# Attention and MLP kernel on one core: transposes moved from TensorE to DMA, a third PSUM bank for the MLP, output drained by VectorE, DMA queues in emission order

## The chip, the cores and the metric

The kernel runs on one core of one Trainium2 chip. The metric is device time in microseconds (us). "Before" is the kernel as it was, "after" is the kernel with the change. Before took 579.5 us (median of three runs, 578.33 to 581.34).

Five engines work beside each other, each on its own instruction list: TensorE (PE in the profile), VectorE (DVE), ScalarE (ACT), GpSimd (POOL) and SyncE (SP). (In before the first four were busy 81, 42, 55 and 37% of the span.) SP computes nothing here. It issues transfers to the core's 16 DMA engines. In these traces VectorE and SP work in the order of their lists, and what stands behind a waiting entry waits with it: in after an `xn` whose inputs were there at 62.1 us started at 73.95, behind a `kp` that waited for its own, and SP issued nothing from 62.9 to 74.5 us, while it waited for that `xn`.

## The reference, cut to what matters

```python
def reference(q, k, v, g_q, g_k, w_in, w_out):     # q, k, v: 8 batches, 12 heads, 448 rows, 64 columns
    q_n, k_n = rmsnorm(q, g_q), rmsnorm(k, g_k)
    attn = softmax(q_n @ k_n.T / sqrt(64))
    x = heads_side_by_side(attn @ v)               # 3584 x 768
    h = x @ w_in                                   # w_in 768 x 2048
    g = h * clip(h + 3, 0, 6) / 6
    return g @ w_out                               # w_out 2048 x 768
```

## The kernel before

Heads are worked on in pairs: 6 pairs a batch, 48 in all. For each pair q and k are loaded with sequence rows on the partitions, squared (`sq`, POOL), summed (`ssq`, VectorE), turned into 1/rms (`rs`, ScalarE) and scaled to bf16 (`qks`, POOL). The kernel's score matmul takes q and k with head columns on the partitions, so `qks` is transposed; k is then multiplied by a mask (`kp`, VectorE), so that one matmul sees one head of the pair. After softmax and the matmul with v, the result `x_ps` is normalised (`xn`, VectorE) and transposed once more (`xT`), because the kernel's MLP takes it with model columns on the partitions. The MLP of batch b−1 (`h`) and of batch b−2 (`y`) is interleaved with the attention of batch b, so that TensorE always has something to do.

The parts that the change touches:

```python
    ps_T = pool("ps_T", 1, space=PSUM)      # transposes
    ps_S = pool("ps_S", 3, space=PSUM)      # scores
    ps_X = pool("ps_X", 1, space=PSUM)
    ps_R = pool("ps_R", 1, space=PSUM)
    ps_M = pool("ps_M", 2, space=PSUM)      # MLP, h and y; 8 banks in these pools
    # ... cut
    def trans_pair(P):
        b, j = divmod(P, NPAIR)
        qks = st.pop(("qks", P))
        ps = ps_T.tile([128, 2, NT, 128], BF16, name="t_ps", tag="T")
        for i in range(2):
            for t in range(NT):
                nc.tensor.transpose(
                    ps[:, i, t, :], qks[:, i, t].rearrange("p h d -> p (h d)"), identity[:])
        nc.vector.tensor_copy(
            out=qT_of(b)[:, j, 0:SM], in_=ps[:, 0].rearrange("p t c -> p (t c)"))
        kp = kp_pool.tile([128, 2, SM], BF16, name="kp")
        for a in range(2):
            nc.vector.tensor_scalar_mul(
                kp[:, a, :], ps[:, 1].rearrange("p t c -> p (t c)"), gmask[:, a:a + 1])
    # ... cut
    def xtrans(P):                          # the attention output of pair P
        xn = st.pop(("xn", P))
        ps = ps_T.tile([128, NT, 128], BF16, name="xt_ps", tag="T")
        for t in range(NT):
            nc.tensor.transpose(ps[:, t, :], xn[:, t].rearrange("p a d -> p (a d)"), identity[:])
        nc.vector.tensor_copy(
            out=xT_of(b)[:, j, 0:SM], in_=ps[:].rearrange("p t c -> p (t c)"))
    # ... cut
        if part == 3:                       # end of y_part
            y_sb = y_pool.tile([128, HALF], FP32, name="y_sb")
            nc.scalar.copy(out=y_sb[:], in_=y_ps)
            # then nc.sync.dma_start(out=..., in_=y_sb)
    # ... cut
    def att_items(P):                       # what is emitted while pair P is finished
        n = P + 1
        items = [(0.0, lambda: load_step(P + 5)), (0.0, lambda: prep_step(P + 3)),
                 (0.36, lambda: trans_step(P + 2))]
        sc = [(0.19, lambda u=u: score(n, u)) for u in range(NU)] if n < NP else []
        vs = [(0.3, lambda t=t: av(P, t)) for t in range(NT + 1)]
        items += merge(sc, vs)
        items.append((0.18, lambda: xtrans(P)))
        # ... cut
    def load_w_in():                        # float32 in HBM, cast to bf16 on the way, issued by POOL
        for kt in range(NKT):
            after(nc.gpsimd.dma_start(
                out=w_in_sb[:, kt, :], in_=moe_w_in[kt * 128:(kt + 1) * 128, :]), st["prep", 1])
```

The order of each engine's list is not the order of emission: the framework simulates the program and sorts the instructions of each engine by when it expects them to be ready.

## Time and profile before

| | before |
|---|---|
| time, median | 579.5 us |
| span of the profiled run, granted TensorE clock | 582.8 us, 0.974 |
| first score exponential | 39.9 us |
| batch starts (first exponential of each batch) | 39.9, 72.8, 115.9, 183.5, 255.8, 325.1, 392.5, 452.7 us |
| first exponential of the last pair | 502.5 us |

The batch starts are read from the timeline: ScalarE takes seven exponentials per pair, and each 42nd starts a batch. A batch is thus a natural ruler for this kernel. First the page: busy time and share of each engine, then TensorE and the DMA engines in 40 slices of the span, in tenths.

```profile
PE 469.9 (81%) x3848; PEld 278.2 (48%) x3848; DVE 245.7 (42%) x544; ACT 320.5 (55%) x638; POOL 212.9 (37%) x245
...
PE   0045859877689888888788899888899999999996
...
DMA  8974995462134222212222123222110000010012
```

No engine is full over the whole span, but TensorE is at 9 in the last quarter, where mostly MLP is left, and at 8 in the middle. Some groups of before's instructions (line, engine, operation, tiles, shapes, count; busy us and mean ns; idle time just before them and what ended it):

```profile
L248 PE MATMUL t_ps<-identity,qks 128*128 128x128 bf16 x288 | 26.1, 228 | 44.6 <-POOL qks L165 41.1
...
L379 ACT COPY y_sb<-y_ps 128x384 f32<-128x384 f32 x56 | 26.8, 479 | 44.0 <-PE y_ps L373 43.9
...
L254 DVE TENSOR_SCALAR kp<-t_ps,gmask 128x384 bf16<-128x384 bf16 x96 | 35.2, 409 | 0.0
```

The 228 ns of one transpose is not its cost: matmuls overlap in the pipeline, and the transposes start 56 ns apart, so 504 of them are worth 28 us of TensorE. What VectorE and TensorE of before wait for (us in all, times, longest):

```profile
DVE ssq L159 <- POOL sq L138: 87.3, 37, 5.5
...
DVE qT L250 <- PE t_ps L248: 26.4, 28, 2.8
```

```profile
PE h_ps L356 <- DVE gT_1641 L363: 10.7, 7, 5.1
```

VectorE's longest wait is for the squares; TensorE's own waits, after the 34.7 us before its first transpose, are many and short. The windows view of before, for the first two batches and the batches after them (length, busy time of each engine with counts, granted clock, DMA share, GB/s):

```profile
core 0: us, PE busy (x) PEld busy (x) DVE busy (x) ACT busy (x) POOL busy (x), PEclk, DMA share, GB/s
40.00:73.00 33.00, 25.11 (x264) 16.12 (x263) 18.62 (x45) 25.12 (x54) 29.30 (x33) 0.90 0.77 165
73.00:116.00 43.00, 33.43 (x337) 20.87 (x336) 30.28 (x68) 33.98 (x81) 37.84 (x38) 0.92 0.73 176
116.00:453.00 337.00, 286.99 (x2369) 169.39 (x2368) 152.72 (x335) 197.28 (x391) 128.99 (x138) 0.97 0.26 75
```

In the first two batches the DMA engines are three quarters busy, not least because the weights arrive there; after that they have room.

### The profile page before, as it was taken

How to read it: one execution, taken by the hardware profiler on the slowest of the kernel's cores; microseconds unless marked ns; L12 is line 12 of the kernel's file. 1: busy time of each engine (PE TensorE's matmuls, PEld its weight loads, DVE VectorE, ACT ScalarE, POOL GpSimd, SP SyncE). 2: the span in 40 equal slices, each digit the busy share in tenths (PEclk: the TensorE clock that was granted, in tenths of full speed). 3: DMA queues.
4: the chain of work that ended last, by engine and by line, in shares of the span. 5: the costliest groups of instructions: out<-in, count | busy, mean ns of one | idle time of the engine just before them, and what ended most of it. 6: DMA issues, size and time to landing. Idle time of an engine off the chain costs nothing.

```text
span 582.8 us, 9889 instructions
## 1 busy us (share of the span) xinstructions
PE 469.9 (81%) x3848; PEld 278.2 (48%) x3848; DVE 245.7 (42%) x544; ACT 320.5 (55%) x638; POOL 212.9 (37%) x245
## 2 busy tenths in 40 slices
PE   0045859877689888888788899888899999999996
PEld 0023535543345555544444455555455566654454
DVE  0035658864544453435543443544443434232200
ACT  1055977865566655636555666555667665733221
POOL 5069769974543532324434353223221100000000
PEclk9997998998999999979998999989999999999999
DMA  8974995462134222212222123222110000010012
GB/s 204 231 149 120 201 236 162 132 154 82 55 86 132 82 70 72 93 54 55 62 77 80 56 82 96 73 64 70 55 55 29 29 28 28 28 42 27 28 56 68
DMA packets 69648, 50.98 MB, mean 87 GB/s; under 512 B 22753, under 2 KB 68833, under 8 KB 69601
## 3 DMA queue, kind: packets, MB, share of 16 engines
q1 hardware_dynamic: 63168, 43.27, 26.4%
q0 software_dynamic: 2976, 6.29, 5.8%
q10 hardware_dynamic: 3456, 0.79, 0.7%
q8 instruction: 30, 0.49, 0.3%
q14 instruction: 18, 0.14, 0.1%
HBM read 45.61 MB, written 11.01 MB: 97 GB/s over the span
## 4 chain that ended last, share of the span: by engine, by line
PE 35%; POOL 23%; DMA 19%; DVE 10%; ACT 5%; issue 4%; SPq 4%; POOLq 0%; ACTq 0%
DMA qk<-in_k_dram 15%; PE h_ps L356 14%; PE y_ps L373 13%; POOL qks L165 9%; POOL sq L138 9%; DVE ssq L159 4%; ACT t_sb L361 3%; PE s_ps L270 3%; SPq L190 2%; PE t_ps L248 2%; SPq L145 2%; POOL sqr L138 1%; DMA vr<-in_v_dram 1%; DMA qkr<-in_k_dram 1%; DVE xn L298 1%
## 5 line engine op out<-in xcount | busy, mean ns | idle before, releaser
L271 ACT ACTIVATE eT<-s_ps,zero_c 128x448 bf16<-128x448 f32 x336 | 200.9, 643 | 52.5 <-PE s_ps L270 50.0
L361 ACT ACTIVATE t_sb<-h_ps,half_c 128x384 f32<-128x384 f32 (+1 forms) x128 | 81.1, 634 | 78.2 <-PE h_ps L356 78.0
L356 PEld LDWEIGHTS <-w_in_sb 128*128 128x128 bf16 x768 | 72.5, 98 | 95.5 <-issue 54.9
L165 POOL TENSOR_TENSOR qks<-qk,rs 128x384 bf16<-128x384 f32 x96 | 77.7, 831 | 103.4 <-PE t_ps L248 71.1
L270 PE MATMUL s_ps<-qT,kp 128*128 128x448 bf16 x288 | 97.1, 360 | 2.5 <-DVE kp L254 1.3
L138 POOL TENSOR_TENSOR sq<-qk 128x768 f32<-128x768 f32 x45 | 66.0, 1468 | 88.4 <-DMA qk<-in_k_dram 80.6
L159 DVE TENSOR_REDUCE ssq<-sq 128x12 f32<-128x768 f32 x48 | 45.7, 952 | 95.7 <-POOL sq L138 87.3
L279 PEld LDWEIGHTS <-eT 128*128 128x128 bf16 x1152 | 66.3, 100 | 30.4 <-issue 2.5
L248 PE MATMUL t_ps<-identity,qks 128*128 128x128 bf16 x288 | 26.1, 228 | 44.6 <-POOL qks L165 41.1
L379 ACT COPY y_sb<-y_ps 128x384 f32<-128x384 f32 x56 | 26.8, 479 | 44.0 <-PE y_ps L373 43.9
L248 PEld LDWEIGHTS <-qks 128*128 128x128 bf16 x288 | 20.9, 101 | 54.1 <-POOL qks L165 41.9
L130 ACT ACTIVATE rs<-ssq,eps_c 128x12 f32<-128x12 f32 x48 | 15.0, 313 | 51.9 <-POOL qks L165 37.3
L356 PE MATMUL h_ps<-xT_984,w_in_sb 128*128 128x512 bf16 x96 | 26.6, 394 | 11.3 <-DVE gT_1641 L363 10.7
L270 PEld LDWEIGHTS <-kp 128*128 128x128 bf16 x288 | 27.9, 99 | 16.3 <-DVE kp L254 1.7
L254 DVE TENSOR_SCALAR kp<-t_ps,gmask 128x384 bf16<-128x384 bf16 x96 | 35.2, 409 | 0.0
L356 PE MATMUL h_ps<-xT_2580,w_in_sb 128*128 128x512 bf16 x96 | 26.5, 389 | 6.9 <-DVE gT_3374 L363 6.7
L373 PE MATMUL y_ps<-w_out_sb,gT_1641 128*128 128x384 bf16 x128 | 28.0, 338 | 1.7 <-ACT y_sb L379 1.6
L373 PE MATMUL y_ps<-w_out_sb,gT_3374 128*128 128x384 bf16 x128 | 27.3, 332 | 1.7 <-ACT y_sb L379 1.6
L356 PE MATMUL h_ps<-xT_1757,w_in_sb 128*128 128x384 bf16 x96 | 22.0, 337 | 7.9 <-DVE gT_2459 L363 7.8
L250 DVE COPY qT<-t_ps 128x384 bf16<-128x384 bf16 x48 | 17.0, 355 | 26.6 <-PE t_ps L248 26.4
L298 DVE TENSOR_TENSOR xn<-x_ps,rd 128x384 bf16<-128x384 f32 x48 | 26.7, 555 | 1.2
L336 PE MATMUL xt_ps<-identity,xn 128*128 128x128 bf16 x144 | 17.3, 226 | 12.1 <-DVE xn L298 11.8
(104 smaller groups left out, 745.5 us busy)
## 6 DMA issues: line engine op xcount, KB each, us to landing
qk<-in_q_dram SPq DMA_DIRECT2D x48, 192.0 KB, 2.5
qk<-in_k_dram SPq DMA_DIRECT2D x48, 192.0 KB, 2.8
vf<-in_v_dram SPq DMA_DIRECT2D x48, 192.0 KB, 2.5
out_dram<-y_sb SPq DMA_DIRECT2D x48, 192.0 KB, 1.9
w_in_sb<-in_moe_w_in_dram POOLq DMA_DIRECT2D x6, 512.0 KB, 11.9
w_out_sb<-in_moe_w_out_dram POOLq DMA_DIRECT2D x4, 768.0 KB, 14.2
vr<-in_v_dram SPq DMA_DIRECT2D x16, 96.0 KB, 6.4
out_dram<-y_sb SPq DMA_DIRECT2D x16, 96.0 KB, 2.2
```

The lines of the kernel that those rows point to most:

```text
L138: nc.gpsimd.tensor_tensor(out=out, in0=x, in1=x, op=A_MULT)
L159: nc.vector.tensor_reduce(out=ssq[:], in_=sq[:].rearrange("p (n d) -> p n d", d=D), axis=AX_X, op=A_ADD)
L165: nc.gpsimd.tensor_tensor(out=qks[:, i].rearrange("p t h d -> p h t d"), in0=qk[:, i].rearrange("p h (t d) -> p h t d", d=D), in1=rs4[:, i ...
L248: nc.tensor.transpose(ps[:, i, t, :], qks[:, i, t].rearrange("p h d -> p (h d)"), identity[:])
L254: nc.vector.tensor_scalar_mul(kp[:, a, :], ps[:, 1].rearrange("p t c -> p (t c)"), gmask[:, a:a + 1])
L270: nc.tensor.matmul(out=ps[:], lhsT=lhsT, rhs=st["qT", b][:, j, :], start=True, stop=True)
L271: nc.scalar.activation(out=st["e", P][:, u, :], in_=ps[:], func=EXP, bias=zero_c[:], scale=1.0)
L279: nc.tensor.matmul(out=dst[:, a * E1:(a + 1) * E1], lhsT=eT[:, u, c0:c0 + 128], rhs=va[:, a, t, :], start=(first and a == 0 and t == 0), s ...
L298: nc.vector.tensor_tensor(out=xn[:], in0=xv[:, :, :, 0:D], in1=rd[:].unsqueeze(3).to_broadcast([128, NT, 2, D]), op=A_MULT)
L356: nc.tensor.matmul(out=h_ps[:, 0:n], lhsT=w_in_sb[:, kt, f * 128:(f + 1) * 128], rhs=st["xT", G][:, kt, :], start=(kt == 0), stop=(kt == N ...
L361: nc.scalar.activation(out=t_sb[:, 0:n], in_=h_ps[:, 0:n], func=RELU, bias=half_c[:], scale=1.0 / 6.0)
L373: nc.tensor.matmul(out=y_ps, lhsT=gT[:, f, i * 128:(i + 1) * 128], rhs=w_out_sb[:, f, nh * HALF:(nh + 1) * HALF], start=(f == 0), stop=(f ...
```

## The change

The intent was to free TensorE of its 504 transposes and of their PSUM bank. The bank goes to the MLP, which then has three; the output copy goes from ScalarE to VectorE, which has fewer drains to do; and SP and POOL issue in the order of emission, so that the weight loads, now spread over several pairs, come where they were written.

```diff
-    ps_T = pool("ps_T", 1, space=PSUM)
-    ps_M = pool("ps_M", 2, space=PSUM)
+    ps_M = pool("ps_M", 3, space=PSUM)
@@ trans_pair (trans_rest likewise, for the last 64 rows of each batch)
-        ps = ps_T.tile([128, 2, NT, 128], BF16, name="t_ps", tag="T")
-        for i in range(2):
-            for t in range(NT):
-                nc.tensor.transpose(...)
-        nc.vector.tensor_copy(out=qT_of(b)[:, j, 0:SM], in_=ps[:, 0]...)
+        nc.sync.dma_start_transpose(
+            out=qT_of(b)[:, j, 0:SM].rearrange("p (t c) -> p t c", t=NT),
+            in_=qks[:, 0].rearrange("p t h d -> p (t h d)"))
+        kT = kT_pool.tile([128, SM], BF16, name="kT")
+        nc.sync.dma_start_transpose(
+            out=kT[:].rearrange("p (t c) -> p t c", t=NT),
+            in_=qks[:, 1].rearrange("p t h d -> p (t h d)"))
         for a in range(2):
-            nc.vector.tensor_scalar_mul(kp[:, a, :], ps[:, 1]..., gmask[:, a:a + 1])
+            nc.vector.tensor_scalar_mul(kp[:, a, :], kT[:], gmask[:, a:a + 1])
@@ xtrans (xtrans_rest likewise)
-        ... three nc.tensor.transpose and a copy by VectorE
+        nc.sync.dma_start_transpose(
+            out=xT_of(b)[:, j, 0:SM].rearrange("p (t c) -> p t c", t=NT),
+            in_=xn[:].rearrange("p t a d -> p (t a d)"))
@@ y_part
-            nc.scalar.copy(out=y_sb[:], in_=y_ps)
+            nc.vector.tensor_copy(out=y_sb[:], in_=y_ps)
@@ weights: no longer tied to an early instruction, but at a place in the order
+    WEIGHTS = {2: [0], 3: [1], 4: [2], 5: [3, 4, 5]}       # slices of w_in after the preparation of these pairs
+    with tc.manual_schedule(engines={mybir.EngineType.SP, mybir.EngineType.Pool}):
         ... the same emission as before, with trans_step of the first two pairs one step sooner
```

All 172 transposes are issued by one engine, SP.

More of the change, by code (lines that the diff above doesn't have):

```diff
@@ L6 @@
 from concourse import bass_utils, mybir
-from concourse.masks import make_identity
 from concourse._compat import with_exitstack
@@ L52 @@
     const = pool("const", 1)
-    identity = const.tile([128, 128], BF16, name="identity")
-    make_identity(nc, identity[:])
     gq_t = const.tile([128, 1], FP32, name="gq_t")
@@ L107 @@
     vr_pool = pool("vr_pool", 2)
+    kT_pool = pool("kT_pool", 3)
     qT_pool = pool("qT_pool", 3)
@@ L223, in trans_rest @@
         qks = st.pop(("qkrs", b))
-        for i in range(2):
-            ps = ps_T.tile([128, NPAIR, 128], BF16, name="tr_ps", tag="T")
-            for j in range(NPAIR):
-                nc.tensor.transpose(
-                    ps[:, j, :], qks[:, i, 2 * j:2 * j + 2, :].rearrange("p h d -> p (h d)"),
-                    identity[:])
-            for e in range(2):
-                part = ps[:, :, e * 64:(e + 1) * 64]
-                if i == 0:
-                    nc.vector.tensor_copy(out=qT_of(b + e)[:, :, SM:S], in_=part)
-                else:
-                    kbd = kbd_pool.tile([128, NPAIR, 128], BF16, name="kbd")
-                    for a in range(2):
-                        nc.vector.tensor_scalar_mul(
-                            kbd[:, :, a * 64:(a + 1) * 64], part, gmask[:, a:a + 1])
-                    st["kbd", b + e] = kbd
+        rT = rst_pool.tile([128, 2, NPAIR, 128], BF16, name="rT")
+        nc.sync.dma_start_transpose(
+            out=rT[:].rearrange("p a j c -> p (a j) c"), in_=qks[:].rearrange("p a h d -> p (a h d)"))
+        for e in range(2):
+            part = rT[:, :, :, e * 64:(e + 1) * 64]
+            nc.vector.tensor_copy(out=qT_of(b + e)[:, :, SM:S], in_=part[:, 0])
+            kbd = kbd_pool.tile([128, NPAIR, 128], BF16, name="kbd")
+            for a in range(2):
+                nc.vector.tensor_scalar_mul(
+                    kbd[:, :, a * 64:(a + 1) * 64], part[:, 1], gmask[:, a:a + 1])
+            st["kbd", b + e] = kbd
     def trans_pair(P):
@@ L244, in trans_pair @@
         qks = st.pop(("qks", P))
-        ps = ps_T.tile([128, 2, NT, 128], BF16, name="t_ps", tag="T")
-        for i in range(2):
-            for t in range(NT):
-                nc.tensor.transpose(
-                    ps[:, i, t, :], qks[:, i, t].rearrange("p h d -> p (h d)"), identity[:])
-        nc.vector.tensor_copy(
-            out=qT_of(b)[:, j, 0:SM], in_=ps[:, 0].rearrange("p t c -> p (t c)"))
+        nc.sync.dma_start_transpose(
[5 more added lines that the diff above has]
+            in_=qks[:, 1].rearrange("p t h d -> p (t h d)"))
         kp = kp_pool.tile([128, 2, SM], BF16, name="kp")
         for a in range(2):
-            nc.vector.tensor_scalar_mul(
-                kp[:, a, :], ps[:, 1].rearrange("p t c -> p (t c)"), gmask[:, a:a + 1])
+            nc.vector.tensor_scalar_mul(kp[:, a, :], kT[:], gmask[:, a:a + 1])
         st["kp", P] = kp
@@ L333, in xtrans @@
         xn = st.pop(("xn", P))
-        ps = ps_T.tile([128, NT, 128], BF16, name="xt_ps", tag="T")
-        for t in range(NT):
-            nc.tensor.transpose(ps[:, t, :], xn[:, t].rearrange("p a d -> p (a d)"), identity[:])
-        nc.vector.tensor_copy(
-            out=xT_of(b)[:, j, 0:SM], in_=ps[:].rearrange("p t c -> p (t c)"))
+        nc.sync.dma_start_transpose(
+            out=xT_of(b)[:, j, 0:SM].rearrange("p (t c) -> p t c", t=NT),
+            in_=xn[:].rearrange("p t a d -> p (t a d)"))
     def xtrans_rest(b, j0):
         xr = st["xr", b // 2]
-        ps = ps_T.tile([128, 3, 128], BF16, name="xtr_ps", tag="T")
-        for i in range(3):
-            nc.tensor.transpose(ps[:, i, :], xr[:, j0 + i, :], identity[:])
-        nc.vector.tensor_copy(out=xT_of(b)[:, j0:j0 + 3, SM:SM + 128], in_=ps[:])
+        for j in range(j0, j0 + 3):
+            nc.sync.dma_start_transpose(out=xT_of(b)[:, j, SM:SM + 128], in_=xr[:, j, :])
     def h_part(G, f, part):
@@ L433, in prep_step @@
             prep_vrest(b)
-        if P == NPAIR:
-            load_w_out()
+        for kt in WEIGHTS.get(P, []):
+            load_w_in(kt)
+        if NPAIR <= P < NPAIR + 4:
+            load_w_out(4 * (P - NPAIR))
     def trans_step(P):
@@ L448, in att_items @@
         items = [(0.0, lambda: load_step(P + 5)), (0.0, lambda: prep_step(P + 3)),
-                 (0.36, lambda: trans_step(P + 2))]
+                 (0.0, lambda: trans_step(P + 2))]
         sc = [(0.19, lambda u=u: score(n, u)) for u in range(NU)] if n < NP else []
@@ L452, in att_items @@
         items += merge(sc, vs)
-        items.append((0.18, lambda: xtrans(P)))
+        items.append((0.0, lambda: xtrans(P)))
         if b % 2 == 1 and j % 3 == 2:
-            items.append((0.18, lambda: xtrans_rest(b, j - 2)))
+            items.append((0.0, lambda: xtrans_rest(b, j - 2)))
         return items
-    def load_w_in():
-        for kt in range(NKT):
-            after(nc.gpsimd.dma_start(
-                out=w_in_sb[:, kt, :], in_=moe_w_in[kt * 128:(kt + 1) * 128, :]), st["prep", 1])
@@ L463, in load_w_out @@
-    def load_w_out():
-        for ft in range(0, NFT, 4):
-            after(nc.gpsimd.dma_start(
-                out=w_out_sb[:, ft:ft + 4, :],
-                in_=moe_w_out[ft * 128:(ft + 4) * 128, :].rearrange("(f p) n -> p f n", p=128)),
-                st["prep", NPAIR])
-    def after(x, y):
-        tc.add_manual_dep(
-            x.ins, y.ins.name,
-            mybir.DependencyInfo(mybir.DependencyClass.NoSync, mybir.DependencyReason.DATA),
-            reason="transfers of weights follow the first inputs")
@@ L476 @@
-    for P in range(5):
-        load_step(P)
-    for P in range(3):
-        prep_step(P)
-        if P == 1:
-            load_w_in()
-    for P in range(2):
-        trans_step(P)
-    for u in range(NU):
-        score(0, u)
-    for b in range(B):
-        att = []
-        for j in range(NPAIR):
-            att += att_items(b * NPAIR + j)
-        mlp = merge(h_items(b - 1) if b >= 1 else [], y_items(b - 2) if b >= 2 else [])
-        for _, fn in merge(att, mlp):
-            fn()
-    for _, fn in merge(h_items(B - 1), y_items(B - 2)):
-        fn()
@@ L496, with load_w_in, load_w_out @@
-    for _, fn in y_items(B - 1):
-        fn()
+    def load_w_in(kt):
+        nc.gpsimd.dma_start(out=w_in_sb[:, kt, :], in_=moe_w_in[kt * 128:(kt + 1) * 128, :])
+    def load_w_out(ft):
+        nc.gpsimd.dma_start(
+            out=w_out_sb[:, ft:ft + 4, :],
+            in_=moe_w_out[ft * 128:(ft + 4) * 128, :].rearrange("(f p) n -> p f n", p=128))
+    WEIGHTS = {2: [0], 3: [1], 4: [2], 5: [3, 4, 5]}
+    with tc.manual_schedule(engines={mybir.EngineType.SP, mybir.EngineType.Pool}):
+        for P in range(5):
+            load_step(P)
+        for P in range(3):
+            prep_step(P)
+            if P < 2:
+                trans_step(P)
+        for u in range(NU):
+            score(0, u)
+        for b in range(B):
+            att = []
+            for j in range(NPAIR):
+                att += att_items(b * NPAIR + j)
+            mlp = merge(h_items(b - 1) if b >= 1 else [], y_items(b - 2) if b >= 2 else [])
+            for _, fn in merge(att, mlp):
+                fn()
+        for _, fn in merge(h_items(B - 1), y_items(B - 2)):
+            fn()
+        for _, fn in y_items(B - 1):
+            fn()
```

## The prediction

The sum of the forecast came to 537 us.

> **What bounds it now.** The page shows PE busy 81% of 582.8 us, ACT 55%, DVE 42%, POOL 37%: no engine is full. Summing, for each kind of matmul in the trace, its shortest usual start-to-start distance (h 162 or 215 ns, y 162, scores 189, values 33 and 56, transposes 56) gives a PE floor of about 430 us, 28 of it the 504 transposes. The timeline has no PE work before 34.7 us, so some 118 us are lost while PE runs. The middle batches (first score exponential to first) take 67 to 72 us for some 54 us of floor. The windows show PE at 82% there and 93 to 99% after 430 us, where mostly MLP is left. So the tail is PE-bound; before it PE waits: h matmuls for the product gT (33 us in all), transposes for xn (12 us). The chain of waits runs through load, square, sum, scaling and PE transposes of each pair.
>
> **The change.**
> 1. 504 PE transposes go: 28 us of floor, near all of it on the critical path, since PE work is conserved. Their PSUM bank and drains (0.35 us x108) leave DVE: 38 us[...].
> 2. The third MLP bank lets h and y run one group further ahead: I credit half of 40 us of bank waits, 20 us.
> 3. y copies (0.48 us x56) go from ACT to DVE at about the same cost: ACT 320 to 294 us, perhaps 5 us gained.
> 4. Startup: ACT's second rest-square waited 17.3 us for a DMA while five w_in loads shared the engines. Now w_in comes later, one slice at a time: 9 us sooner to the first score.
> 5. Added: 172 DMA transposes, 16.5 MB. [...] No trace here shows one; plain 256-byte packets took 18 ns. I guess 1 to 2 us of issue on SP and 3 to 5 us to landing for 384 columns. q and k are issued a pair (10 us) ahead, so this should hide; at batch starts the first h waits for the last xT, perhaps 2 us x7 = 14 us lost. In-order SP, waiting for y and xn before the next transposes, may lose 5 us more.
>
> Sum: 580 - 28 - 20 - 5 - 9 + 14 + 5 = 537 us. Range 497 to 605. Faster 0.66, within 2% 0.13, slower 0.21.
>
> **What would show it.** 3344 PE matmuls (504 fewer); first score before 30 us; middle batches near 61 us; h waits for gT under 20 us; DVE busy near 210 us, ACT near 294 us; transposes landing in under 5 us, DMA share under 60% in the middle; last exponential near 455 us, then a dense PE tail.
>
> **What would make it wrong.** SP needing over 2.5 us for a transpose, or DMA engines full: then scores wait for kp, kp for DMA, batches reach 75 us, and the time passes 600. Transposes queueing behind 5 pairs of loads, so that the first score is no sooner. xT landing late, PE idling at batch starts. The other way: if emission order lets PE run near its floor, 500 us.

## The result, and the profile after

| | before | after |
|---|---|---|
| time, median (range), four runs each | 579.41 us (578.33 to 581.34) | 622.07 us (618.91 to 625.62) |
| ratio after/before (95% interval) | | 1.0734 (1.0664 to 1.0804): slower |
| span of the profiled run, granted clock | 582.8 us, 0.974 | 623.8 us, 0.901 |

A ratio here and below is the mean time of a kernel's fast runs over that of before's fast runs of the same rounds, so it is not quite the ratio of the medians. One per cent of before is 5.8 us; where kernels of different rounds are compared, the ratios are subtracted and turned into us with this figure. On one core a run counts as slow when it is over 1.5% above the fastest of the same kernel.

The page of after:

```profile
PE 461.5 (74%) x3344; PEld 257.1 (41%) x3344; DVE 253.5 (41%) x496; ACT 302.8 (49%) x582; POOL 212.8 (34%) x243
...
PE   0065234676579777969798989596988789789997
...
DMA  9498665994444245444353538343434332120012
```

TensorE has 504 instructions fewer, as intended. Yet it is at 2 to 7 in the slices of the first two batches (30 to 161 us). The windows view of after, for the first two batches and the middle:

```profile
30.00:88.00 58.00, 27.75 (x223) 15.55 (x222) 17.86 (x38) 25.28 (x51) 23.93 (x29) 0.79 0.73 138
88.00:161.00 73.00, 42.74 (x317) 23.35 (x317) 26.93 (x57) 35.55 (x76) 32.18 (x34) 0.78 0.74 142
161.00:484.00 323.00, 268.85 (x1994) 149.19 (x1992) 152.49 (x294) 186.55 (x358) 136.91 (x146) 0.92 0.44 113
```

With the batch starts as a ruler the span of every kernel splits into five stretches. These are the ledgers of before and after, in us:

| stretch | before | after | difference |
|---|---|---|---|
| start to first exponential | 39.9 | 30.3 | −9.6 |
| batches 1 to 3 | 143.6 | 185.9 | +42.3 |
| batches 4 to 7 | 269.2 | 267.6 | −1.6 |
| batch 8, to its last pair | 49.8 | 59.2 | +9.4 |
| last pair and MLP tail | 80.3 | 80.8 | +0.5 |
| span | 582.8 | 623.8 | +41.0 |

(Batches 1 to 3 are taken together because after does some 36 MLP matmuls in its first two batches which before does in its third.) The loss is in the first three batches, and 9.4 us of it in batch 8. The middle, which was to shrink by a tenth with 28 us of transposes gone, hardly moved.

What VectorE and SP of after wait for, and then TensorE:

```profile
DVE kp L246 <- DMA kT<-qks: 130.6, 39, 11.4
...
DVE ssq L156 <- POOL sq L135: 22.8, 19, 4.2
```

```profile
SPq L370 <- DVE y_sb L366: 127.8, 35, 7.8
```

```profile
PE s_ps L261 <- DVE kp L246: 34.2, 21, 7.7
...
PE h_ps L343 <- DVE y_sb L366: 26.6, 8, 6.2
PE x_ps L270 <- DVE xn L289: 17.5, 4, 11.4
PE h_ps L343 <- DMA xT_380<-xn: 10.2, 4, 5.5
```

In before VectorE stood 26.4 us for the transposes, before the copy `qT`, and not at all before `kp`. Now it stands 130.6 us before `kp`. Of TensorE's waits only the first names `kp`. But the waits for `y_sb` and `xn` are of the same kind: both are VectorE instructions, and they share VectorE's one order with `kp`. The two groups of after that answer to those shown of before:

```profile
L246 DVE TENSOR_SCALAR kp<-kT,gmask 128x384 bf16<-128x384 bf16 x96 | 43.0, 489 | 130.6 <-DMA kT<-qks 130.6
...
L366 DVE COPY y_sb<-y_ps 128x384 f32<-128x384 f32 x56 | 30.8, 551 | 20.4 <-PE y_ps L360 20.2
```

The transposes themselves look harmless. The view of the tile `kT` in after says how long SP needs to issue one (shortest, median, longest in ns), and how long it takes from there to its landing:

```profile
L241 SPq DMA_TRANSPOSE kT<-qks x48: 1189/1200/2713, 24.0 to 531.9; - x48
...
DMA to landing us min/median/max: 2.3/2.4/12.5
```

The median is 2.4 us, the longest 12.5. Here is that longest one in after's timeline (start, duration, instruction; in brackets the idle time before it and what ended it; rows of other instructions left out):

```profile
60.51 1.66 POOL L448 DMA_DIRECT2D w_in_sb<-in_moe_w_in_dram  x3
...
61.00 1.94 SPq L241 DMA_TRANSPOSE kT<-qks  x1
...
73.48 0.55 DVE L246 TENSOR_SCALAR kp<-kT,gmask 128x384 bf16<-128x384 bf16 x2 [11.41 <-DMA kT<-qks]
73.95 0.55 DVE L289 TENSOR_TENSOR xn<-x_ps,rd 128x384 bf16<-128x384 f32 x1
74.53 1.18 SPq L325 DMA_TRANSPOSE xT_380<-xn  x1
...
74.56 0.29 PE L270 MATMUL x_ps<-va_81,eT 128*128 128x65 bf16 x2 [11.44 <-DVE xn L289]
```

POOL issues three slices of `w_in` at once, half a microsecond before SP issues the transpose of `kT`. The transpose lands 12.5 us later. VectorE stands before `kp` all that time, although the next instruction in its order, `xn`, has had its data since 62 us. TensorE waits for `xn`, which frees the PSUM bank of the next pair, and SP waits for `xn` too.

In the middle there are no weights, and one turn looks like this (after's timeline again, SP, VectorE and POOL):

```profile
216.08 0.56 DVE L289 TENSOR_TENSOR xn<-x_ps,rd 128x384 bf16<-128x384 f32 x1
...
217.14 0.55 DVE L366 COPY y_sb<-y_ps 128x384 f32<-128x384 f32 x1
...
217.72 0.36 SPq L370 DMA_DIRECT2D out_dram<-y_sb  x1
218.14 1.20 SPq L325 DMA_TRANSPOSE xT_1599<-xn  x1
...
219.38 0.57 SPq L142 DMA_DIRECT2D qk<-in_q_dram  x1
...
221.08 1.18 SPq L237 DMA_TRANSPOSE qT<-qks  x1
222.35 1.20 SPq L241 DMA_TRANSPOSE kT<-qks  x1
...
224.83 1.81 DVE L246 TENSOR_SCALAR kp<-kT,gmask 128x384 bf16<-128x384 bf16 x2 [4.30 <-DMA kT<-qks]
```

Read it as a chain. `xn` and the copy `y_sb` are done by VectorE; then SP stores y, issues the transpose of `xn`, three loads, the transposes of q and of k, and about 2.4 us later VectorE can do `kp`. Only after that does VectorE's order let it do the next `xn`. From the first `xn` to `kp` it is 8.8 us, and here `kp` follows `kp` at 214.52, 224.83 and 236.50 us, 10.3 and 11.7 us apart. This is a loop, one pair per turn. That the transposes were emitted two pairs ahead does not help: the next pair's `xn` stands behind this `kp`. A second path runs beside it: the `ssq` of the next pair (217.61) also stood behind the last `kp`, and the `qks` that follows from it is ready at 220.93, just before SP issues the transpose of q. SP itself issues almost without a pause from 217.72 to 223.55 us, 5.8 us of the turn.

Little was left of the lead. Taking each pair in the trace of after, the first score matmul began 5.2 us (median) after SP issued the transpose of its k, and in 25 of 48 pairs less than 0.2 us after the first of its `kp` was done. In before the median from that `kp` to the score was 8.7 us.

### The profile page after: what moved, and what is told of

It reads as the page before. It is cut to its first block, busy times and chain, and to the rows that moved or that the text cites. A ratio compares the mean times of both kernels' runs of the same rounds, so it can differ in the third digit from the quotient of the medians.

```text
span 623.8 us, 9051 instructions
## 1 busy us (share of the span) xinstructions
PE 461.5 (74%) x3344; PEld 257.1 (41%) x3344; DVE 253.5 (41%) x496; ACT 302.8 (49%) x582; POOL 212.8 (34%) x243
## 4 chain that ended last, share of the span: by engine, by line
issue 37%; POOL 24%; PE 16%; DMA 12%; SPq 6%; DVE 3%; POOLq 0%; ACT 0%; ACTq 0%
POOL sq L135 9%; PE y_ps L360 9%; POOL qks L162 8%; PE h_ps L343 6%; DMA kT<-qks 5%; SPq L332 3%; DMA qkr<-in_k_dram 2%; POOL vbd_89 L194 1%; POOL vbd_92 L194 1%; SPq L237 1%; PE s_ps L261 1%; SPq L325 1%; POOL sqr L135 1%; DMA qk<-in_k_dram 1%; POOL vbd_95 L194 1%
## 5 line engine op out<-in xcount | busy, mean ns | idle before, releaser
L262 ACT ACTIVATE eT<-s_ps,zero_c 128x448 bf16<-128x448 f32 x336 | 203.6, 635 | 158.7 <-PE s_ps L261 157.5
L261 PE MATMUL s_ps<-qT,kp 128*128 128x448 bf16 x288 | 112.3, 407 | 65.1 <-DVE kp L246 34.2
L343 PEld LDWEIGHTS <-w_in_sb 128*128 128x128 bf16 x768 | 75.4, 102 | 109.5 <-issue 57.1
L246 DVE TENSOR_SCALAR kp<-kT,gmask 128x384 bf16<-128x384 bf16 x96 | 43.0, 489 | 130.6 <-DMA kT<-qks 130.6
L270 PEld LDWEIGHTS <-eT 128*128 128x128 bf16 x1152 | 69.1, 104 | 58.8 <-DVE xn L289 18.7
L261 PEld LDWEIGHTS <-kp 128*128 128x128 bf16 x288 | 30.2, 107 | 112.4 <-DVE kp L246 72.0
L366 DVE COPY y_sb<-y_ps 128x384 f32<-128x384 f32 x56 | 30.8, 551 | 20.4 <-PE y_ps L360 20.2
L343 PE MATMUL h_ps<-xT_896,w_in_sb 128*128 128x512 bf16 x96 | 28.3, 395 | 8.4 <-DVE y_sb L366 5.0
L343 PE MATMUL h_ps<-xT_380,w_in_sb 128*128 128x384 bf16 x96 | 25.0, 378 | 12.5 <-DMA xT_380<-xn 10.2
L343 PE MATMUL h_ps<-xT_2374,w_in_sb 128*128 128x512 bf16 x96 | 28.2, 402 | 5.3 <-DMA xT_2374<-xr 4.2
L343 PE MATMUL h_ps<-xT_1599,w_in_sb 128*128 128x384 bf16 x96 | 22.3, 340 | 12.6 <-DVE y_sb L366 9.6
L343 PE MATMUL h_ps<-xT_3983,w_in_sb 128*128 128x512 bf16 x96 | 27.8, 397 | 4.3 <-DMA xT_3983<-xr 2.8
L343 PE MATMUL h_ps<-xT_5596,w_in_sb 128*128 128x512 bf16 x96 | 27.2, 406 | 3.1 <-DMA xT_5596<-xr 3.1
L343 PE MATMUL h_ps<-xT_4817,w_in_sb 128*128 128x384 bf16 x96 | 21.9, 337 | 8.7 <-DVE y_sb L366 5.4
L343 PE MATMUL h_ps<-xT_3208,w_in_sb 128*128 128x384 bf16 x96 | 22.1, 337 | 7.9 <-DVE y_sb L366 6.6
```

The source lines that it names most:

```text
L246: nc.vector.tensor_scalar_mul(kp[:, a, :], kT[:], gmask[:, a:a + 1])
L261: nc.tensor.matmul(out=ps[:], lhsT=lhsT, rhs=st["qT", b][:, j, :], start=True, stop=True)
L262: nc.scalar.activation(out=st["e", P][:, u, :], in_=ps[:], func=EXP, bias=zero_c[:], scale=1.0)
L270: nc.tensor.matmul(out=dst[:, a * E1:(a + 1) * E1], lhsT=eT[:, u, c0:c0 + 128], rhs=va[:, a, t, :], start=(first and a == 0 and t == 0), s ...
L343: nc.tensor.matmul(out=h_ps[:, 0:n], lhsT=w_in_sb[:, kt, f * 128:(f + 1) * 128], rhs=st["xT", G][:, kt, :], start=(kt == 0), stop=(kt == N ...
L366: nc.vector.tensor_copy(out=y_sb[:], in_=y_ps)
```

## The experiments

The theory after these readings was that the DMA transposes are the loss. They are slow neither in themselves nor because the DMA engines are full, but because VectorE's fixed order has `kp` before `xn`, so that a late `kT` holds up the very instructions from which SP's next transfers follow. Beside the weight loads the landing becomes long as well. The rivals were these: the weight loads alone are at fault; SP is simply overloaded with issues; the lead of the transposes is too short; or another part of the change (the y copy on VectorE, the order of emission, the banks) costs the time. Where a quoted expectation uses a letter for a theory, it means the one whose consequence that sentence states. Every kernel gives the reference's result, unless it is said to be wrong. All edits are against after, unless another kernel is named.

All the runs in one table (before was timed on the same chip each time, in seven runs; its medians there were 581.6 to 583.1 us):

| run | what | median us | ratio to before (95%) |
|---|---|---|---|
| (after) | the change | 622.07 | 1.0734 (1.0664 to 1.0804) |
| e1_pe_all | all transposes back on TensorE, 2 MLP banks | 565.48 | 0.9703 (0.9664 to 0.9741) |
| e2_lead | loads, preparation, transposes a pair sooner | 606.97 | 1.0419 (1.0371 to 1.0466) |
| e3_no_weights | no weight loads | 592.96 | 1.0184 (1.0131 to 1.0237) |
| e4_loads_pool | q, k, v loads issued by POOL | 662.82 | 1.139 (1.1345 to 1.1436) |
| e5_psm2 | 2 MLP banks | 655.2 | 1.1299 (1.1223 to 1.1374) |
| f1_kp_late | `kp` later in VectorE's order | 582.19 | 0.9931 (0.985 to 1.0012) |
| f3_x_on_pe | only x back on TensorE, 2 banks | 608.9 | 1.0463 (1.0434 to 1.0492) |
| f4_qk_on_pe | only q, k back on TensorE, 2 banks | 582.09 | 0.9998 (0.9961 to 1.0035) |
| f2_no_weights | f1 without weight loads | 551.38 | 0.9478 (0.9426 to 0.9531) |
| f7_small_packets | f1 with weights in small packets | 586.81 | 1.0061 (1.0013 to 1.011) |
| g1_pe_3banks | e1 with 3 MLP banks, 2 for scores | 548.62 | 0.9426 (0.9397 to 0.9454) |
| g2_pe_y_act | e1 with y on ScalarE | 577.92 | 0.992 (0.9868 to 0.9971) |
| h1_pe_twice | g1 with each transpose done twice | 573.97 | 0.9856 (0.9827 to 0.9885) |
| h2_kp_after_ssq | one half of f1's order | 617.26 | none: three of four runs slow |
| h3_kp_after_xn | the other half of f1's order | 593.11 | 1.0188 (1.0156 to 1.022) |

### Undo the transposes alone: e1_pe_all

```diff
-        nc.sync.dma_start_transpose(...)                 # all of them
+        nc.tensor.transpose(...)                         # as in before, with VectorE's drains
+    ps_T = pool("ps_T", 1, space=PSUM)
-    ps_M = pool("ps_M", 3, space=PSUM)
+    ps_M = pool("ps_M", 2, space=PSUM)
```

> The changed kernel with all transposes back on PE (one PSUM bank for them, two for the MLP); emission order, weights spread over pairs and y on VectorE stay. Theory A (the DMA transposes are the loss): 560 to 590 us, first two batches (first score exponential of batch 0 to that of batch 2) near 76 us as in the kernel before, not 131. Rival B (in-order SP and POOL queues are the loss): 610 us or more, first two batches over 110 us.

It took 565.48 us, ratio 0.9703. (The third MLP bank goes too, since the transposes need theirs; e5 below accounts for it.) The y copy on VectorE and the emission order are still in it, so together they are a gain, and the loss of after lies in the transposes. In the ledger, batches 1 to 3 take 152.2 us, against 185.9 in after, and batches 4 to 7 take 252.8, against 267.6. The first two batches took 87.4 us, nearer to the 76 expected than to 131, but not the 76.

### The bank taken back: e5_psm2

```diff
-    ps_M = pool("ps_M", 3, space=PSUM)
+    ps_M = pool("ps_M", 2, space=PSUM)
```

> The changed kernel with two PSUM banks for the MLP instead of three, the others unused. The prediction credited the third bank with 20 us. Where the transposes set the pace it should be worth little: 620 to 632 us. If it does carry 20 us: 638 us or more.

Without the third bank the time is 655.2 us (one of its four runs was slow and is not in the ratio). The third bank was thus worth 5.65% of before, 33 us, where I had credited 20. Comparing e5 with e1 isolates the transposes at equal banks: 1.1299 against 0.9703, or 93 us for moving them off TensorE.

### More lead: e2_lead

```diff
-        items = [(0.0, lambda: load_step(P + 5)), (0.0, lambda: prep_step(P + 3)),
-                 (0.0, lambda: trans_step(P + 2))]
+        items = [(0.0, lambda: load_step(P + 6)), (0.0, lambda: prep_step(P + 4)),
+                 (0.0, lambda: trans_step(P + 3)), (0.0, lambda: fin_step(P + 2))]   # fin_step: kp alone
     # ... cut: one buffer more for kT and for v; the weights stay at their pairs
```

> The changed kernel with loads, preparation and the q/k transposes issued one pair earlier, the kp multiplies left where they were in VectorE's order. Theory A1 (per pair a loop: xn, then SP's xT, three loads and the q and k transposes, landing, kp in VectorE's line ahead of the next xn): waits of kp for kT fall from 131 us to under 40 us, time to 590 us or less. Rival A2 (the DMA engines or SP's issue time are full): kp waits on, time stays within 2% of 622 us.

It gained 3.2% against after, but the wait that was to vanish is still there. In the waits of VectorE in e2:

```profile
DVE kp L254 <- DMA kT<-qks: 133.9, 38, 10.0
```

So neither branch of the expectation came: the wait stayed, and the gain is over 2%. In the trace TensorE has its lead back: from the issue of `kT` to the pair's first score it is now 12.9 us (median; 5.2 in after), and that score begins 10.1 us after its `kp`. But VectorE still stands in line for transfers that nobody needs yet. The framework, which orders VectorE by its own simulation, saw `kT` earlier and moved part of the `kp` forward: in 18 of 48 pairs `kp` now stands before the `xn` of three pairs earlier, in after in none. The run gained 18 us in all, so a longer lead is not the remedy. What has to be held is the place of `kp` in VectorE's order.

### Hold the place of `kp`: f1_kp_late, h3_kp_after_xn, h2_kp_after_ssq

```diff
         for a in range(2):
-            nc.vector.tensor_scalar_mul(kp[:, a, :], kT[:], gmask[:, a:a + 1])
+            i = nc.vector.tensor_scalar_mul(kp[:, a, :], kT[:], gmask[:, a:a + 1])
+            for before in (("xn_i", P - 2), ("ssq_i", P + 1)):     # h3: the first alone, h2: the second alone
+                if before in st:
+                    order(i, st[before])                           # an order on VectorE, no data
```

The same two instructions are now emitted after `xtrans`, and tied behind the `xn` of two pairs earlier and the `ssq` of the next pair. (At batch starts the copies and masked copies of the last 64 rows move with them.) SP, POOL, transfers and work stay as they were.

> The changed kernel, transposes issued at the same places; only VectorE's order is tied: the kp multiplies of pair P+2 come after xn of pair P and after the sum of squares of pair P+3. In the run with a lead the kp multiplies had moved forward in VectorE's order and waited for the newest transpose again, so that run did not test the wait. Theory A1 (VectorE stands in line behind a transpose, and the next pair's sum of squares, which the next transpose needs, stands behind it): waits of kp for kT fall from 131 us to under 45 us, middle batches from 65 to 71 us to 62 or less, time 570 to 598 us. Rival A2 (SP's issue and the engines set the pace): kp waits fall, others take their place, time over 610 us.

f1 took 582.19 us, ratio 0.9931 (two of its four runs, 582.87 and 585.04, count as slow beside its fastest of 574.1, and are not in the ratio). By the ratios the place of two instructions in VectorE's list was worth 8.0% of before, 47 us; by the medians it was 40. VectorE's wait before `kp` fell, though not to the 45 us expected, and the longest landing did not fall:

```profile
DVE kp L254 <- DMA kT<-qks: 73.3, 30, 9.1
```

```profile
DMA to landing us min/median/max: 2.3/2.4/16.0
```

(The second line is of the view of tile `kT` in f1.) Batches 4 to 7 take 248.1 us, against 267.6 in after, and batch 8 takes 47.7, against 59.2: here most of the loss of the loop is gone. SP issues as much as in after (173 us in batches 4 to 7, 171 in after), so SP's issue time alone did not set the pace there. Batches 1 to 3 still take 173.1.

> The other tie alone: kp of pair P+2 after xn of pair P, free against the sum of squares. In the built order the sum of squares of pair P+3 mostly comes first all the same. If xn is what must not stand behind a transpose: within 1.5% of 582 us. If the tie to the sum of squares is needed: 600 us or more.

h3 took 593.11 us, ratio 1.0188: the tie to `xn` alone gives 32 of the 47 us. It is a little above the range expected of it.

> The run with kp tied late (582 us), with one of the two ties: kp of pair P+2 after the sum of squares of pair P+3, free against xn. If the loop through the next pair's preparation is the costly one: within 1.5% of 582 us. If the loop through xn and the transpose of the attention output is: 605 us or more.

h2 took 606.19 to 621.41 us; three of its four runs count as slow beside the fourth, so it has no ratio. Its fastest run is 24 us over f1's median. Without a ratio I read from its time no more than that the tie to `ssq` alone does not do what the two ties do. The built orders can be counted in the traces: `kp` stands before the `xn` of two pairs earlier in 27 of 48 pairs in after, in 17 in h2, and in none in h3 and f1, while the order of `ssq` and `kp` in h3 is that of after. So h3 changed the order to `xn` alone and got most of the gain: the costly coupling is the one between `kp` and `xn`, the instruction that SP's next transfers wait for. Before has this order in 46 of 48 pairs without the loss; only with the transposes by DMA is there a long wait at `kp`.

### Take only one kind of transpose back: f3_x_on_pe, f4_qk_on_pe

```diff
     # f3: xtrans and xtrans_rest on TensorE as in before; q and k stay with the DMA; ps_T 1, ps_M 2
     # f4: trans_pair and trans_rest on TensorE as in before; x stays with the DMA; ps_T 1, ps_M 2
```

> The changed kernel with the attention output transposed on PE again (one bank for it, two for the MLP), q and k by DMA. Theory A1 (the q and k transposes carry the loss): within 15 us of 622 us. Rival A2 (number of DMA transposes, SP time): a third of them gone, 595 to 605 us.

> The changed kernel with q and k transposed on PE again (one bank, two for the MLP), the attention output by DMA. Theory A1: 560 to 578 us, near the 565 us of all transposes on PE. Rival A2: 582 us or more.

With e1 (both on TensorE) and e5 (both by DMA) these make a square at two MLP banks. Moving q and k to the DMA costs 44 us where x is on TensorE (f3 against e1) and 76 us where x is on the DMA (e5 against f4). Moving x costs 17 us (f4 against e1) or 49 us (e5 against f3). The two don't add up: both together cost 93, not 61. The loop would explain this, since it closes only where the transposes of `xn` and of k stand in the same SP order. The ledger agrees for the middle: batches 4 to 7 take 252.8 us in e1, 258.2 in f3, 261.3 in f4, and 284.1 in e5. The expectations, written for three banks and one culprit, do not fit well: f4's 582.09 us is at the rival's line (582 or more) and not in 560 to 578, and f3's 608.9 is within 15 us of after but 46 below its partner e5. In f3 the rest of the loss, 32 of its 44 us, sits in batches 1 to 3 (184.6 us against 152.2), where the weights arrive.

### The weights: e3_no_weights, f2_no_weights, f7_small_packets

e3 is after, and f2 is f1, without any weight load; a constant is written to the weight tiles at the start instead. Their results are wrong.

```diff
+    nc.vector.memset(w_in_sb[:], 0.03)          # f2: by nc.gpsimd, so that the start is not held up
+    nc.vector.memset(w_out_sb[:], 0.02)
     def load_w_in(kt):
-        nc.gpsimd.dma_start(out=w_in_sb[:, kt, :], in_=moe_w_in[kt * 128:(kt + 1) * 128, :])
+        pass                                    # load_w_out likewise
```

> Wrong on purpose: weights are constants set by VectorE, nothing of them is loaded. Theory C (weight loads on the same 16 engines delay the transposes in the first two batches): these two batches shrink from 131 us to under 105 us, the whole to under 597 us. Rival (the loop alone): under 10 us gained in all.

e3 took 592.96 us, 5.5% or 32 us less than after, although its constants delayed the first exponential to 39.4 us. Batches 1 to 3 fell from 185.9 to 145.8 us, while batches 4 to 7 stayed at 265.8: without weights the loop is still there. That these batches, whose MLP uses the constants too, did not gain speaks against the constants themselves as the reason.

> Wrong on purpose: the run with kp tied late, and no weights loaded (constants set by POOL and VectorE at the start). Theory: two separate causes. What is left of the loss in the first two batches (117 us against 76 us in the kernel before) is the weight loads beside the transposes: 117 falls to 95 us or less, landing of kT in them under 5 us at most, whole 550 to 563 us. Rival: the first two batches are slow for another reason and stay over 105 us.

f2 took 551.38 us, ratio 0.9478, which is 26 us less than f1 by the ratios and 31 by the medians. Batches 1 to 3 fell from 173.1 to 138.0, and batches 4 to 7 stayed (248.1 and 250.7). So each of the two causes has mainly its own stretch. The landing of `kT` in f2:

```profile
DMA to landing us min/median/max: 2.3/2.4/4.5
```

The longest went from 16.0 us in f1 to 4.5. Whether it is the bytes or the packets of the weights that delay the transposes, f7 tries. It is f1 with the weights cut by columns (`w_in` in eight pieces instead of six, issued after the same four preparations), so that a packet of `w_in` is 512 bytes in SBUF and not 4096, and one of `w_out` 384 and not 1536:

```diff
-    def load_w_in(kt):
-        nc.gpsimd.dma_start(out=w_in_sb[:, kt, :], in_=moe_w_in[kt * 128:(kt + 1) * 128, :])
+    def load_w_in(c):
+        n = slice(c * 256, (c + 1) * 256)
+        nc.gpsimd.dma_start(
+            out=w_in_sb[:, :, n], in_=moe_w_in[:, n].rearrange("(k p) n -> p k n", p=128))
```

> The run with kp tied late, and the same weight bytes in smaller packets: w_in in 8 column blocks (rows of 512 bytes after the cast instead of 4096), w_out in 4 (384 bytes instead of 1536). A 4096-byte packet took 322 ns and a transpose's 256-byte packet 18 ns; if an engine takes turns by packet, a transpose beside w_in goes at a small part of its pace. Theory (turns by packet): longest landing of kT falls from 16 us to under 8 us, first two batches from 117 to 105 us or less, whole to 572 us or less. Rival (bytes alone): no change over 1%, or slower from more packets.

```profile
DMA to landing us min/median/max: 2.3/2.4/6.4
```

The longest landing fell to 6.4 us. What a large packet does to the small ones can be seen in the packet records of after, for the transpose of `kT` that SP issued at 61.0 us and that landed 12.5 us later. Between 65 and 70 us 250 packets of 256 bytes started (median 31 ns) and 232 of 4096 bytes, which are `w_in`'s (322 ns): about one for one, as over the whole transfer (387 and 373 from 62.5 to 73.5 us). Between 75.5 and 76.5 us, with no `w_in` packets, 384 of 256 bytes started, as many as one transpose of 384 columns has (98,304 bytes). This fits turns by packet between the two transfers; which engine moved a packet the records do not say. Over all of after the medians are 324 ns for a packet of `w_in` and 18 ns for one of 256 bytes. But the time was not gained: 586.81 us, ratio 1.0061. The first batch got shorter (56.3 to 51.2 us), the second longer (60.3 to 73.9), perhaps because the same weights in small packets took 54 us of every DMA engine instead of 41 in f1. The landings (16.0 us in f1, 6.4 in f7) support the theory of turns; the remedy is no remedy.

### Is SP overloaded? e4_loads_pool

```diff
-            nc.sync.dma_start(
+            (nc.sync if P < 5 else nc.gpsimd).dma_start(
                 out=qk[:, i], in_=...)                       # the load of v likewise
```

> The changed kernel with the q, k and v loads from pair 5 on issued by POOL instead of SP. Theory A1 (SP's issue time, about 0.5 us for each of three loads, lies in the loop of each pair): 1 to 1.5 us a pair less from pair 12 to 42, 25 to 45 us in all. Rival (landing and DMA engines set the pace): within 1% of 622 us, or slower since POOL spends 0.6 us on each issue.

It took 662.82 us (two of five runs slow, left out of the ratio of 1.139), 38 us worse than after. I had expected a gain. In e4's timeline POOL now issues loads just ahead of its squares:

```profile
254.19 0.75 POOL L142 DMA_DIRECT2D qk<-in_q_dram  x1
...
254.94 0.72 POOL L142 DMA_DIRECT2D qk<-in_k_dram  x1
255.66 0.72 POOL L145 DMA_DIRECT2D vf<-in_v_dram  x1
...
256.40 1.48 POOL L135 TENSOR_TENSOR sq<-qk 128x768 f32<-128x768 f32 x1
```

Issuing the three loads takes POOL 2.2 us per pair, and POOL has the squares, at the head of the next pair's chain, right behind them. But the ledger puts the loss elsewhere: batches 1 to 3 take 216.6 us, against 185.9 in after, and batches 4 to 7, from which this timeline is, 270.8, against 267.6. In batches 1 to 3 POOL issues the weights as well; there the loads of q and k landed 4.7 us (median) after their issue, against 2.8 in after, and `kT` 5.1 us, against 2.4. Why they landed later is not shown. In batches 4 to 7 SP spent 138 us on issues, 33 less than in after, and no time was gained. Together with f1, which got faster with all of SP's issues in place, this speaks against an overloaded SP as the cause, though e4 changes POOL at the same time. The time to issue is not small: in after, 1.2 us of issue against 2.4 us to landing for a transpose on SP, and 0.41 to 0.57 us (medians) for a load of q, k or v; in e4, 0.72 to 0.75 us for such a load on POOL.

### What the other parts are worth, and a version that beats both: g1_pe_3banks, g2_pe_y_act, h1_pe_twice

All three have the transposes on TensorE. g1 takes the third MLP bank from the scores instead of from the transposes:

```diff
     # against e1
-    ps_S = pool("ps_S", 3, space=PSUM)
+    ps_S = pool("ps_S", 2, space=PSUM)
-    ps_M = pool("ps_M", 2, space=PSUM)
+    ps_M = pool("ps_M", 3, space=PSUM)
```

> All transposes on PE as in the first experiment (565 us), with three PSUM banks for the MLP and two for the scores instead of two and three. If the third MLP bank is worth as much here as in the changed kernel (33 us) and the scores need no third: 535 to 550 us. If scores and exponentials need their third bank: 565 us or more. Expected between: 555 us.

g1 took 548.62 us, ratio 0.9426: 16 us better than e1, and the fastest kernel with a correct result. Its page:

```profile
PE 465.8 (85%) x3848; PEld 280.2 (51%) x3848; DVE 274.2 (50%) x600; ACT 304.1 (55%) x582; POOL 212.6 (39%) x245
...
PE   0277678867889999699989999699989999999996
```

TensorE is at 9 in most slices from about 165 us on, with all the transposes on it.

g2 takes the y copy back to ScalarE, in e1:

```diff
-            nc.vector.tensor_copy(out=y_sb[:], in_=y_ps)
+            nc.scalar.copy(out=y_sb[:], in_=y_ps)
```

> All transposes on PE, y copies back on ScalarE: what is left of the change is the emission order and the timing of the weights. If the 3% of the first experiment came from the order and the weights: 565 us within 1%. If from y on VectorE: 578 us or more.

577.92 us, ratio 0.992. Against e1 the copy on VectorE is worth 2.2%, about 13 us. What remains between g2 and before, 0.8% or 5 us, is the emission order with the later weights (a difference within the 2% that count as the same).

h1 is g1 with every transpose done twice, into the same place. This measures what 504 transposes cost where TensorE is the bound:

```diff
             for t in range(NT):
-                nc.tensor.transpose(ps[:, i, t, :], ...)
+                for twice in range(2):
+                    nc.tensor.transpose(ps[:, i, t, :], ...)
```

> The best kernel so far (all transposes on PE, three MLP banks, 548.6 us) with each of the 504 PE transposes issued twice into the same place: 28 us more of PE floor, the result unchanged, nothing more for VectorE. The prediction's step: 28 us of PE floor are near all on the critical path. If so, 548.6 becomes 570 us or more. If PE has room in the batches: under 560 us.

573.97 us against 548.62, 4.3% or 25 us. The 28 us of floor that the prediction worked out from the starts 56 ns apart are real time: nine tenths of them lie on the critical path of this kernel.

## Why the prediction was wrong

The prediction was 537 us with a range of 497 to 605; the time was 622. The step that failed is in its point 5: **"q and k are issued a pair (10 us) ahead, so this should hide"**, together with the price put on it, 14 us at batch starts and 5 us for in-order SP. Instead the first score came 5.2 us (median) after the issue of its k transpose, VectorE stood 130.6 us before `kp`, and the waits cost about 100 us instead of 19. The terms of its sum against what the runs measured:

| term of the sum | predicted | measured | by |
|---|---|---|---|
| 504 transposes off TensorE | −28 | 25 us where TensorE is the bound; not visible in after, which is not bound there | h1 |
| third MLP bank | −20 | −33 in after, −16 with transposes on TensorE | e5, g1 |
| y copy on VectorE | −5 | −13 with transposes on TensorE | g2 |
| start | −9 | −9.6 (first exponential at 30.3 us) | after |
| waits on DMA transposes and SP | +19 | about +100 | g1, h1 |

The last figure is an estimate: after stands 13.1% or 76 us above g1, which has the transposes on TensorE, three MLP banks and y on VectorE as well; add the 25 us that h1 gives for the transposes' own time. (g1 has one score bank less, so the pair is not perfectly matched.) The runs divide it as follows.

**Shown: the order of VectorE.** About 47 us are the place of `kp` in VectorE's order (f1), of which 32 come back with the tie to `xn` alone (h3). The lead of one pair was there in the order of emission, but two in-order lists used it up. VectorE's list has `kp` of a later pair before `xn` of an earlier one, and SP's list has the transpose of that `xn`, and three loads, before the next transposes of q and k. So a late transfer holds up the engine that has to feed the next transfer. e2 shows the same from the other side: there the lead was 12.9 us, and VectorE still stood 133.9 us before `kp`, for results that TensorE needed only some 10 us later. The square of e1, f3, f4 and e5 shows that most of the loss in the middle appears only when both kinds of transposes go by DMA; that it is SP's list that couples them is argued from the timeline.

**Shown: the weights beside the transposes.** Removing the weight loads gives back 26 to 32 us, in batches 1 to 3 (f1 to f2, after to e3), and takes the longest landing of `kT` from 16.0 to 4.5 us. In before the weights arrived in the same stretch, but nothing that TensorE needed at once came by DMA from SBUF. The prediction counted the later weights only as a gain of 9 us at the start. That gain came, and the same loads then stood beside the first batches' transposes.

**Left over.** f2, which has neither the weights nor the worst of the order, takes about as long as g1 (551 and 549 us), although TensorE has 504 transposes less to do. In f2's list of waits TensorE still stands 28 us for `kp` and about 20 us for `xT`. So even at its best here, what was gained on transposes seems to have gone into waits; the two kernels differ in score banks and weights too, so this is not a measurement. No run has the DMA transposes without any wait.

Now the single claims of the prediction:

- Right, or nearly: 3344 matmuls. The first exponential came at 30.3 us, against "before 30 us". h waits for `gT` are 10.3 us in all (predicted under 20), but h now waits 26.6 us for `y_sb`. ScalarE is busy 302.8 us (294). DMA share in the middle is 0.44 (under 0.60), so full DMA engines, one of the risks named, were not the reason.
- Right, but not decisive: the transposes as such. They were guessed at 1 to 2 us of issue and 3 to 5 us to landing, and after shows 1.2 and 2.4 us at the median for `kT` (3.3 us to landing for `qT`). In the packet records of after, 256-byte packets took 107.5 us of every engine, 64,512 of these 79,872 being the transposes', which is 87 us for their 16.5 MB, or 190 GB/s (an estimate from the packet records). Neither the landings nor this explains the loss: with the same transposes f1 is 47 us faster.
- Right in kind: "scores wait for kp, kp for DMA, batches reach 75 us, and the time passes 600" is what happened in the second batch (73.6 us). But it was expected only if SP needed over 2.5 us for a transpose or the DMA engines were full. Neither was so at the median.
- Wrong: middle batches near 61 us (after: 66.9 us on average over batches 4 to 7; f1, with the order mended: 62.0). The last exponential near 455 us (after: the last pair starts at 543). Transposes landing in under 5 us: nearly true in the middle (at most 4.2 us for `kT`, 5.2 for `qT`), not beside the weights (12.5).
- Wrong: VectorE busy near 210 us; it was 253.5. The drains that left were worth 37 us, as counted, and the y copies added 31. The error is `kp`: the forecast counted on a shorter one (no trace then showed a `kp` that reads SBUF), and it measured 489 ns in the mean, more than the 409 ns of before. The tile views of before and after show the spread (shortest, median, longest in ns):

```profile
L254 DVE TENSOR_SCALAR kp<-t_ps,gmask x96: 406/409/417, 37.2 to 493.6; 128x384 bf16<-128x384 bf16 x96
```

```profile
L246 DVE TENSOR_SCALAR kp<-kT,gmask x96: 305/320/1518, 26.3 to 534.6; 128x384 bf16<-128x384 bf16 x96
```

  Sorting after's 96 instructions by whether POOL was computing at the same time, the 58 that ran alone took 314 ns on average (at most 321), and the 38 beside a POOL instruction took 756 ns (at most 1518). In before, 87 of 96 ran beside POOL and took 409 ns all the same; there they read PSUM. So here an operation moved from PSUM to SBUF got slower on average (409 to 489 ns), though alone it was faster (314). Why it is slow beside POOL was not shown. The 38 slow ones cost after about 17 us of VectorE's busy time (38 times 0.44 us, an estimate). What that costs in time was not tried.

**Open.** The granted clock was 0.901 in after and 0.974 in before. It was lowest where TensorE stood still most (0.78 and 0.79 in the first two batches), and in g1 (0.964) and f2 (0.965 in the profiled run) it is higher again. In batches 4 to 7 it was 0.92 in after and 0.97 in f1, where only VectorE's order had changed, so the clock moved with the waits. No run separates the two, so I can't say how much of the loss is the clock's. Why part of the `kp` wait (73.3 us in f1) remains after the order is mended, how much SP's own issue time adds to the loop, and whether the weights can be loaded beside DMA transposes without delaying them, are open too; f7 tried one way, without success. No run has both the longer lead of e2 and the order of f1.

## What to carry to other kernels

Where work moved from a busy engine to a transfer, its latency (2.4 us at the median) and its lead said little by themselves. Look at the position of the instruction that receives it in its engine's order, and at what stands behind it: if the next transfer is fed from there, latency turns into a loop with a period of its own (here 10.3 and 11.7 us for the turns that were read). Keep bulk loads out of the stretch in which small transfers are waited for at once: the longest landing of `kT` was 16.0 us with the weight loads (f1) and 4.5 us without them (f2). And test the parts of a bundled change singly: here the bank, the copy and the order of emission were worth 33 us together with transposes left on TensorE (548.6 us, g1), and the part that gave the change its name cost more than that.
